# One line of transfers for two steps at once, gates turned by VectorE, and a new order of the first chunk in an mLSTM cell with a leaky-ReLU feed-forward

## The chip, the cores and the metric

The kernel runs on one core of a Trainium2 chip. The metric is the device time of one execution in microseconds (us); 484.99 us is the median of three runs of the kernel before. A core has five engines, each with an instruction stream of its own that it works through in order: TensorE (PE; loads of its weights are listed apart, as PEld), VectorE (DVE), ScalarE (ACT), GpSimd (POOL) and SyncE (SP). SyncE only gives out transfers; ScalarE can give them out too. Sixteen DMA engines carry them.

## The reference

```python
# q, k, v, o_gate: (4, 8, 768, 40); i_gate, f_gate: (4, 8, 768), all float32
for t in range(S):
    m_new = np.maximum(f_gate[:, :, t] + m, i_gate[:, :, t])
    f_stab = np.exp(f_gate[:, :, t] + m - m_new)
    i_stab = np.exp(i_gate[:, :, t] - m_new)
    C = f_stab * C + i_stab * outer(v_t, k_t)          # per batch and head, 40 x 40
    n = f_stab * n + i_stab * k_t
    h_tilde = C @ q_t
    denom = np.maximum(np.abs(n @ q_t), 1.0)
    y[:, :, t] = sigmoid(o_gate_t) * h_tilde / denom
x = y.transpose(0, 2, 1, 3).reshape(3072, 320)
h = x @ w_in                                           # w_in: 320 x 2048, float64
out = np.maximum(0.01 * h, h) @ w_out                  # w_out: 2048 x 320, float64
```

The recurrence is an attention with decays, so that it can be worked in chunks: scores inside a chunk, and a state that carries the earlier ones.

## The kernel before, in words

**Tiling.** The 768 tokens are cut into six chunks c of 128; a chunk has four steps, one for each batch entry, so there are 24 steps, s = 4c + b, of 128 tokens by 8 heads. The feed-forward of a chunk's 512 tokens is a *group* g; the loop over c runs the cell of chunk c together with group c - 1. Chunk 0 and the start of group 0 are written out in `first_chunk` (L1124). From L1244 on, a loop goes through the units of the group (`ffs`; 28 a chunk from group 1 on, 32 in group 0) and puts the parts of the cell between them at places given by lists (`place`, `first_pairs`, `pairs`, L1235 to L1239): `u_parts` (scores and state), `u_plain` (chunk 1) or `u_mix` (chunks 2 to 5; output of a step), `u_gates` (turned gates) and `u_x` (turned x, chunk 1). Group 0 multiplies in full (L812, L834); groups 1 to 5 multiply in blocks with fewer products (L976, L869).

**Order.** TensorE, VectorE, ScalarE and GpSimd run in the order in which the program names their instructions (`manual_schedule`, L1215). SyncE does not: class `Ordered` (L90) ties each transfer to the one before it only while `order["on"]` is true, that is to the end of the loads at L1229; after it every transfer is only behind that last one, and a planner orders them.

**Weights.** w_in and w_out come as 64-bit floats. `load_weights` (L234) fetches a raw block (n = 0 to 3: w_in; 4 to 11: two rows of blocks of w_out each) and `narrow_weights` (L269) makes 32-bit floats of it in six instructions: two on ScalarE (L277, L278), four on VectorE (L279 to L286). Unit j of group 0 needs block j // 2 of w_in. In the opening, blocks 0 and 1 are narrowed whole.

**Opening.** Transfers, in order: gates, then k, q, v of steps 0 and 1, block 0, o of steps 0 and 1, gates of chunk 2, k and q of steps 2 and 3, block 1, v and o of steps 2 and 3. The work of a step of chunk 0: exponentials of the gate biases that TensorE sums (L443, L459; L468, L477), turned k and q (`u_transpose`, L597, L600), scores (L609, L613), values (L700), denominators, tanh of the output gate (`prep_o`, L530), gating (L709, L713), turned x (`u_x`, L800 to L802) and the state (L621, L629). Two units of group 0 (`ffs[0]`, `ffs[1]`) stand in the midst of it.

**Gates.** `gates` (L295) scans the gates of a chunk on VectorE, `gates_exp` (L323) makes exponentials and writes the decays to DRAM (`a_dr`), `gates_T` (L346) turns them on TensorE (tile tg; L350, and L355 for the decays at the ends of the halves, spread over all partitions) and copies them with VectorE (L357, L359).

**Transfers of chunks 2 to 5.** A step's k, q and o are fetched in four transfers each (`load_blocks`, L401) into `rb_t[s % 2]`, its decays in two into `ea` (`spread_q`, L429, two buffers), all as soon as the step two before has used its own (`load_next`, L536). `u_mix` writes x of a step to DRAM in four transfers (L774) and `gather_x` (L777) fetches it back into xT in eight. k, the decay mask w and the four pieces of v of a step four ahead are given out by ScalarE, one behind each unit (`feed_slowly`, L1102). For chunk 1, `feed` (L1095) does it on SyncE.

Of the kernel before, what the change touches and what calls it, by code (L numbers as in the profile page):

```python
# [19 lines left out]
def kernel(  # L20
# [28 lines left out]
    P = 128  # L49
# [13 lines left out]
    TS = SL // QW  # L63
    RL = PR * TB * D
    RW = RL + 2 * QW
# [9 lines left out]
    SLOTS = ([0, 2, 4, 1, 3], [1, 3, 0, 2, 4])  # L75
# [13 lines left out]

    class Ordered:  # L90
# [4 lines left out]
        def dma_start(self, to, part):  # L95
            ins = self.eng.dma_start(to, part).ins  # L96
            if "at" in order:
                tc.add_manual_dep(ins, order["at"], ISSUED, reason="issue order")
            if order["on"]:
                order["at"] = ins.name  # L100

# [7 lines left out]
    for r in range(RG):  # L109
        nc.scalar.dma_start(f0[ts(r, BH), :], f_all[:, :P])  # L110
        sync.dma_start(i0[ts(r, BH), :], i_all[:, :P])
    fi = {}

    def load_fi(c):
        t = fi[c] = wk.tile([BH, 2, P], F32, name="fi")
        eng = nc.scalar if c < 2 else sync
# [22 lines left out]
    NR = 2  # L139
    EAB = 2  # L140
# [4 lines left out]
    rb_t = [consts.tile([P, 3, RW], F32, name=f"rb{n}") for n in range(NR)]  # L145
# [27 lines left out]
    def prepare_tiles():  # L173
# [4 lines left out]
        for t in rb_t:  # L178
            nc.gpsimd.memset(t[:, :, RL:], 0.0)

# [23 lines left out]
    def run_of(r, at):  # L204

        ks = SLOTS[r][at:]
        return ks[0], next((i for i in range(1, len(ks)) if ks[i] != ks[i - 1] + 2), len(ks))
# [26 lines left out]
    def load_weights(n, half=None):  # L234
# [7 lines left out]
        if half == 1:  # L242
            to = raws[n][0] if wide else dst
        elif wide:
# [12 lines left out]
        if n < QN:  # L257
            src = moe_w_in[:, n * QC : (n + 1) * QC].rearrange("(k p) (r c) -> r p k c", p=DP, r=2)
            for at, n_k in ((0, 2), (3, 2), (2, 1)):
                for r in range(2) if half is None else (half,):  # L260
                    k0 = SLOTS[r][at]
                    rows = to[DP * r : DP * (r + 1), 2 * P * at : 2 * P * (at + n_k)].rearrange("p (k c) -> p k c", k=n_k)
                    part = src[r, :, k0 : k0 + 2 * n_k - 1 : 2, :]
# [5 lines left out]
    def narrow_weights(n):  # L269
# [3 lines left out]
        raw, dst = raws.pop(n)  # L273
        words = raw.bitcast(U32).rearrange("p (c two) -> p c two", two=2)
        lo, hi = words[:, :, 0], words[:, :, 1]
        d = dst.bitcast(U32)
        yield nc.scalar.activation(dst, hi.bitcast(F32), AF.Abs)  # L277
        yield nc.scalar.activation(lo, lo, AF.Copy, scale=2.0**-29)  # L278
        yield nc.vector.tensor_scalar(  # L279
# [6 lines left out]
        yield nc.vector.tensor_tensor(d, d, lo, op=ALU.add)  # L286
# [3 lines left out]
    x_dr = dr.tile([NS, Dm, P], F32, name="x_dr")  # L290
# [32 lines left out]
    def gates_exp(c):  # L323
# [10 lines left out]
        if c > 0:  # L334
            sync.dma_start(a_dr[c, 0].rearrange("u n t -> n u t"), a[:].rearrange("n (u t) -> n u t", u=2))
            if c > 1:
                sync.dma_start(a_dr[c, 1].rearrange("u n t -> n u t"), bu[:, 2, :].rearrange("n (u t) -> n u t", u=2))
            if 1 < c < NB - 2:
# [1021 lines left out]
```

## Time and profile before

| | us |
|---|---|
| median of the three runs | 484.99 (484.12 to 487.19) |
| the profiled execution, its own time | 481.97 |
| its span, first to last instruction | 480.2 |
| TensorE busy | 463.2 |
| VectorE, ScalarE, GpSimd busy | 332.0, 203.9, 164.7 |
| DMA queues' share of 16 engines: SyncE's (q1), ScalarE's (q10) | 47.8%, 9.2% |

The profile is of one execution. Each digit of a row of slices is the busy share of a fortieth of the span (12 us) in tenths; PEclk is the clock granted to TensorE in tenths. The chain that ended last is followed back from the last instruction, step by step, to what released it. A timeline row has start, time, engine, line, operation, tiles and, in brackets, how long the engine idled before it and what ended that. L12 is line 12 of the kernel before.

### The profile page before, as it was taken

The numbers are of one execution on the slowest core, as the hardware profiler recorded it, in microseconds if no ns is written. First come the engines' busy times: TensorE is split into PE (matmuls) and PEld (weight loads), VectorE is DVE, ScalarE is ACT, GpSimd is POOL, SyncE is SP. The second block draws the span as 40 slices with busy tenths as digits, with TensorE's granted clock in tenths as the row PEclk, the third lists the DMA queues.
The fourth block names the chain that finished last, engine by engine and source line by source line (L and its number), as shares of the span: only waits on it lengthen the run. The fifth ranks groups of instructions, "written<-read, shape, count | busy, mean of one in ns | idle before, by whom it ended". The sixth has DMA issues, their size and how long they took to land.

```text
span 480.2 us, 14140 instructions
## 1 busy us (share of the span) xinstructions
PE 463.2 (96%) x5715; PEld 418.3 (87%) x5715; DVE 332.0 (69%) x588; ACT 203.9 (42%) x488; POOL 164.7 (34%) x201
## 2 busy tenths in 40 slices
PE   7586999999999999999999999999999999999997
PEld 6475888777788999988899988899988899988997
DVE  4668576798939998878698768689757686104631
ACT  3662598864336621347520446411357411153210
POOL 4232405552362333854115943114733004400020
PEclk9888899999999999999999999999999999999999
DMA  9999776968761593675673875754776112100001
GB/s 117 168 196 222 134 205 141 266 122 180 165 151 29 143 184 73 154 165 131 167 143 85 175 160 116 188 110 108 172 156 133 48 37 75 63 1 1 8 9 42
DMA packets 165329, 59.31 MB, mean 124 GB/s; under 512 B 128592, under 2 KB 156048, under 8 KB 165264
## 3 DMA queue, kind: packets, MB, share of 16 engines
q1 hardware_dynamic: 125232, 51.23, 47.8%
q10 hardware_dynamic: 40032, 7.18, 9.2%
q8 instruction: 45, 0.74, 0.6%
q14 instruction: 20, 0.16, 0.1%
HBM read 51.68 MB, written 6.70 MB: 122 GB/s over the span
## 4 chain that ended last, share of the span: by engine, by line
PE 87%; DVE 4%; SPq 4%; DMA 2%; POOL 1%; issue 1%; ACT 1%; ACTq 0%; DVEq 0%; POOLq 0%
PE ph L976 33%; PE po L869 32%; PE po L834 7%; PE ph L812 6%; SPq L96 4%; PE pT L753 3%; PE sd L665 3%; PE sd L671 1%; DMA qn<-in_q_dram 1%; DMA fi<-in_f_gate_dram 1%; PE hN L725 1%; DVE w_in L286 1%; DVE w_out L286 1%; PE tk L583 0%; DVE w_out L285 0%
## 5 line engine op out<-in xcount | busy, mean ns | idle before, releaser
L869 PE MATMUL po<-w_out,acts 128*128 128x160 f32 x640 | 89.1, 300 | 0.0
L869 PEld LDWEIGHTS po<-w_out,acts 128*128 128x128 f32 x640 | 87.3, 190 | 0.6 <-ACT acts L1001 0.3
L976 PE MATMUL ph<-xT,w_in 64*128 64x256 f32 x720 | 82.7, 378 | 0.0
L976 PEld LDWEIGHTS ph<-xT,w_in 64*128 64x128 f32 x720 | 69.2, 187 | 8.6 <-issue 0.6
L869 PE MATMUL po<-raw,acts 128*128 128x160 f32 x480 | 66.4, 300 | 0.0
L1005 DVE TENSOR_TENSOR acts<-acts,ph 128x512 f32<-128x512 f32 x60 | 38.4, 683 | 39.8 <-PE ph L976 39.6
L869 PEld LDWEIGHTS po<-raw,acts 128*128 128x128 f32 x480 | 65.4, 190 | 0.3
L641 POOL TENSOR_TENSOR S<-S,f 40x336 f32<-40x336 f32 x36 | 31.1, 864 | 67.0 <-PE pT L753 33.2
L1009 ACT COPY acts<-ph 128x512 f32<-128x512 f32 x60 | 32.2, 588 | 46.4 <-PE ph L976 46.4
L1001 ACT ACTIVATE acts<-acts 128x1024 f32<-128x1024 f32 x30 | 31.7, 1057 | 43.8 <-DVE acts L1005 40.5
L494 ACT ACTIVATE w<-w,gT 128x64 f32<-128x64 f32 x160 | 41.9, 340 | 11.3 <-POOL vu L514 3.6
L682 DVE TENSOR_TENSOR qn<-w,sd 64x384 f32<-64x384 f32 (+1 forms) x80 | 33.4, 418 | 16.4 <-ACT acts L1009 7.3
L486 POOL TENSOR_TENSOR w<-w,i 128x512 f32<-128x512 f32 x20 | 27.1, 1366 | 50.7 <-DMA w<-a_dr 23.7
L812 PE MATMUL ph<-xT,w_in 64*128 64x256 f32 x320 | 38.8, 396 | 1.6 <-DVE w_in L286 1.6
L812 PEld LDWEIGHTS ph<-xT,w_in 64*128 64x128 f32 x320 | 32.8, 196 | 5.4 <-ACT kqT L600 1.2
L834 PE MATMUL po<-w_out,acts 128*128 128x320 f32 x128 | 36.7, 437 | 0.0
L976 PE MATMUL ph<-acts,w 64*128 64x256 f32 x320 | 36.3, 379 | 0.0
L767 POOL TENSOR_TENSOR xb<-xb,den 128x320 f32<-128x320 f32 x16 | 11.6, 728 | 67.6 <-DVE xb L764 67.6
L976 PEld LDWEIGHTS ph<-acts,w 64*128 64x128 f32 x320 | 30.6, 187 | 3.6
L907 POOL TENSOR_TENSOR y<-y,raw 128x160 f32<-128x160 f32 x10 | 12.9, 1291 | 57.2 <-ACT y L906 57.2
L834 PEld LDWEIGHTS po<-w_out,acts 128*128 128x128 f32 x128 | 23.5, 190 | 9.2 <-issue 0.3
L557 DVE TENSOR_TENSOR qn<-kqT,ea 64x512 f32<-64x512 f32 x32 | 29.3, 917 | 0.8
(175 smaller groups left out, 721.1 us busy)
## 6 DMA issues: line engine op xcount, KB each, us to landing
rb<-in_k_dram SPq DMA_DIRECT2D x64, 80.0 KB
rb<-in_q_dram SPq DMA_DIRECT2D x64, 80.0 KB
rb<-in_o_gate_dram SPq DMA_DIRECT2D x64, 80.0 KB
ea<-a_dr SPq DMA_DIRECT2D x32, 128.0 KB
raw<-in_moe_w_out_dram SPq DMA_DIRECT2D x6, 640.0 KB
w<-a_dr ACTq DMA_DIRECT2D x24, 128.0 KB
xT<-x_dr SPq DMA_DIRECT2D x32, 96.0 KB
x_dr<-x SPq DMA_DIRECT2D x64, 40.0 KB
```

What stands on the lines that cost most here:

```text
L486: nc.gpsimd.tensor_tensor(w, w, cm2.unsqueeze(1).to_broadcast([P, H, SL]), op=ALU.add)
L494: yield nc.scalar.activation(w[:, h, :], w[:, h, :], AF.Exp, bias=gT[c][:, 0, bh : bh + 1], scale=1.0)
L557: nc.vector.tensor_tensor(mixed(s)[rows, 1 - r], d["kqT"][rows, 1].rearrange("p (h t) -> p h t", t=SL), d["ea"][rows], op=ALU.mult,)
L641: nc.gpsimd.tensor_tensor(new, old, g, op=ALU.mult)
L682: nc.vector.tensor_tensor(mixed(s)[toks, u, hs], w[toks, hs], bank[1 - u][to[u][hs.start], hs], op=ALU.mult,)
L812: nc.tensor.matmul(ph[r][:, cols], lhsT=w_row(r, slot, j), rhs=xT[DP * r : DP * (r + 1), slot, cols], start=(slot == 0), stop=(slot == KC ...
L834: nc.tensor.matmul(po[n][:], lhsT=acts[:, f, ts(n, P)], rhs=w_out[:, f, :], start=(f == 0), stop=(f == NF - 1),)
L869: nc.tensor.matmul(bank[:], lhsT=left[:, f, :], rhs=right[:, f, :], start=f == 0, stop=f == KH - 1)
L976: nc.tensor.matmul(bank[r][:, e, :], lhsT=left(r)[rows, e], rhs=right(r)[rows], start=first and e == 0 and m == 0, stop=e == 1 and m == le ...
L1001: nc.scalar.activation(to, z, AF.Prelu, alpha=0.01)
L1005: nc.vector.tensor_tensor(to[:, 2 * r : 2 * r + 2], to[:, 2 * r : 2 * r + 2], bank[r], op=ALU.add)
L1009: nc.scalar.copy(to[:, 2 * r : 2 * r + 2], bank[r])
```

## The change

Six things are done together.

1. **Two steps at once.** `rb` is one tile that holds k, q and o of two steps side by side. `load_blocks` fetches both steps in one transfer, when the second of them (odd s) asks; `spread_q` fetches `ea` for both, into one buffer; x of two steps goes to a common DRAM block and comes back in three transfers (the slots of xT are renumbered so that neighbours are contiguous). `feed_pair` replaces `feed_slowly`: k and w of two steps in one transfer each, the eight pieces of v as before.
2. **All on SyncE, in source order.** `order["on"]` stays true from chunk 2 on as well; ScalarE gives out transfers only at the very start. So that the order fits, `later(units, fn)` writes a transfer so many units behind the place in the source where it was: the stores of x two, the gathers four or one, the output's stores one, the gates' two, the loads of a pair one. In chunks 0 and 1 it does nothing.
3. **Gates turned by VectorE.** For chunks 2 to 5 `turn_gates` turns two kinds of gates by four 32-wide turns of VectorE; the decays at the halves' ends go through DRAM (`g_dr`) and are fetched for all partitions by `spread_decays`. Chunk 1 keeps `gates_T`. `u_gates` is gone from the list of cells.
4. **First chunk.** Its steps are cut into small ones (`turn`, `turned`, `scores`, `scaled`, `values`, `dens`, `gated`, `normed`, `ends`, `flip`, `flipped`, ...) that run in the order of one long string. Blocks 0 and 1 of w_in are narrowed in two halves each (by `e`, so that a unit needs one half), their low words on ScalarE into a place of their own (`narrow_low`). Three units of group 0 stand in it instead of two. Six warming matmuls at the start are gone, four and two stand further on. Some gating moves to GpSimd. The transfers are in a new order, given before the rest.
5. **Group 0.** A new order of transfers for chunk 1, with v of steps 4 to 7 in one transfer each to a place in `acts` from which GpSimd copies the halves (`split_v`); new places of the cells; a list of how many narrowing instructions run at each unit (`now`).
6. **Chunk 2.** Slightly other places of cells, of the mixed weights and of the gates (`pr`, `mix`, `ga`, `ge`).

The diff, cut to its core:

```diff
-    SLOTS = ([0, 2, 4, 1, 3], [1, 3, 0, 2, 4])
+    SLOTS = ([0, 1, 2, 3, 4], [1, 2, 3, 4, 0])
...
+    def later(units, fn):
+        if unit[0] is None or units == 0:
+            fn()
+        else:
+            due.append((unit[0] + units, fn))
...
-            if "at" in order:
-                tc.add_manual_dep(ins, order["at"], ISSUED, reason="issue order")
             if order["on"]:
+                if "at" in order:
+                    behind(ins, order["at"])
                 order["at"] = ins.name
+            else:
+                behind(ins, order["at"])
...
-    rb_t = [consts.tile([P, 3, RW], F32, name=f"rb{n}") for n in range(NR)]
+    rb = consts.tile([P, 3, RW], F32, name="rb")
...
+    def low_part(n, e):
+        at = (WC // 2 * e, 4 * HW * 2)[n]
+        return raw_l[:, at : at + WC // 2].bitcast(U32).rearrange("p (k c) -> p k c", k=KC)
+    def narrow_low(n, e):
+        words = raws[n][0].bitcast(U32)
+        lo = words.rearrange("p (k e c two) -> p k e c two", k=KC, e=2, two=2)[:, :, e, :, 0]
+        nc.scalar.activation(low_part(n, e), lo, AF.Copy, scale=2.0**-29)
...
+    def spread_decays(c):
+        to = f0[:, ts(c % 2, 2 * BH)]
+        sync.dma_start(to, g_dr[c].rearrange("n u -> (n u)").partition_broadcast(P))
+        gL[c] = to.rearrange("p (n u) -> p u n", u=2)
+    def turn_gates(c):
+        bu = bus.pop(c)[0]
+        g = gT[c] = wk.tile([P, 3, BH], F32, name="gT")
+        for j in range(P // BH):
+            nc.vector.transpose(g[ts(j, BH), :2, :], bu[:, :2, ts(j, BH)])
...
+    def split_v(s):
+        halves = staged(s).rearrange("p (h k d) -> p h k d", k=2, d=DB)
+        for u in range(2):
+            nc.gpsimd.tensor_copy(S_v[s % NL][ts(u, SL), u, :, :, :DB], halves[ts(u, SL)])
...
-        elif s < NS:
-            load_blocks(s, i)
+        elif s < NS and s % NR:
+            load_blocks(s - 1, i)
...
-        src = (k, q, o_gate)[i][b, :, ts(c, P), :]
+        src = (k, q, o_gate)[i][b : b + NR, :, ts(c, P), :].rearrange("b h p d -> (b h) p d")
...
+        if s % NR == 0:
+            return
...
-        d["ea"] = wk.tile([P, H, SL], F32, name="ea", bufs=EAB)
+        ea = wk.tile([P, NR * H, SL], F32, name="ea", bufs=1)
...
-        if s + NR < NS:
+        def fetch():
             load_late(s + NR, 0)
             load_late(s + NR, 1)
             if s + NR >= 2 * B:
                 spread_q(s + NR)
+        if s + NR < NS:
+            later(1, fetch)
...
+        later(2, out_x)
...
-        src = x_dr[s].rearrange("(k p) t -> p k t", p=DP)
+        src = x_dr[s // NR].rearrange("(k p) m t -> p k (m t)", p=DP)
...
-            send(n, 1)
+            later(0 if last else 1, lambda: send(n, 1))
...
-    def feed_slowly(steps):
...
+    def feed_pair(s, eng):
...
+        yield eng.dma_start(
+            kn[:, n : n + NR, :, :D].rearrange("p m h d -> p (m h) d"),
+            k[b : b + NR, :, ts(c, P), :].rearrange("b h p d -> p (b h) d"),
+        )
+        for m in range(NR):
+            for u in range(2) if m else ():
+                yield eng.dma_start(
+                    w_all[ts(u, SL), n : n + NR, : H * SL],
+                    a_dr[c, 0, u, b * H : (b + NR) * H, :].rearrange("(m h) t -> m (h t)", m=NR).partition_broadcast(SL),
+                )
...
+    ORDER = "gates:0 masks:0 gexp:0 terms:0 exps:0:1 gT:0 gates:1 exps:0:1 exps:0:1 exps:0:1 masks:1 vu:0 turn:0:0 turn:1:0 turn:0:1 turned:0:0:v turned:0:1:s turned:1:0:s scores:0 turn:1:1 scaled:0:0 terms:1 exps:1:2 exps:1:2 exps:1:2 scaled:0:1 narrow:0:1:1 o:0 turned:1:1:v scores:1 scaled:1:0 low:0:0 scaled:1:1 values:0 values:1 narrow:0:0:1 gexp:1 gated:0 dens:0 o:1 dens:1 normed:0:v ends:0:s narrow:0:0:1 flip:0 gated:1 normed:1:g exps:1:2 begin warm:4 narrow:0:1:1 flipped:0:1:s narrow:0:1:1 narrow:0:0:1 turn:2:0 exps:1:2 ends:1:g narrow:0:0:1 vu:1 turned:2:0:v tiles flipped:0:0:s narrow:0:0:1 step:1 low:0:1 flip:1 turn:2:1 exps:1:2 exps:1:2 flipped:1:0:s flipped:1:1:v narrow:0:1:1 turned:2:1:s turn:3:0 ff:0 narrow:0:1:1 exps:1:2 scores:2 turn:3:1 turned:3:1:s state:0 low:1:1 state:1 narrow:1:0:1 scaled:2:1 low:1:0 scaled:2:0 turned:3:0:v vu:2 step:0 kept:0 scores:3 kept:1 narrow:1:0:1 values:2 o:2 narrow:1:1:1 narrow:1:0:1 gT:1 vu:3 ff:1 gated:2 scaled:3:0 narrow:1:1:1 scaled:3:1 warm:2 dens:2 normed:2:g narrow:1:1:1 narrow:1:0:1 ends:2:g narrow:1:0:1 o:3 values:3 step:2 dens:3 flip:2 gated:3 normed:3:g ends:3:s ff:2 flip:3 narrow:1:1:1 flipped:2:0:s state:2 flipped:2:1:s flipped:3:0:s step:3 state:3 narrow:1:1:1 kept:3 kept:2 flipped:3:1:s".split()
...
+        for line in "0:1 1:0 0:0 1:1 0:2 8:0 1:2 0:3 2:0 1:3 2:2 2:1 3:1 3:0 3:3 8:1 2:3 3:2 9:2".split():
+            n, i, *at = map(int, line.split(":"))
+            if n == 9:
+                load_fi(i)
+            elif n == 8:
+                load_weights(i, *at)
+            else:
+                load_first(n, i)
         ffs = first_chunk()
...
+        for line in "f:5:0 l:4:2 l:4:1 w:2 f:4:1 f:5:1 l:5:1 f:4:0 f:4:2 w:3 f:7:1 w:4 f:5:2 f:6:1 f:7:0 f:6:0 w:5 w:6 f:7:2 l:5:2 f:6:2".split():
...
+        Z = {'nff': 3, 'fetch': {7: (3,), 9: (5, 6), 10: (4,), 16: (7,)}, 'place': (6, 8, 11, 12, 14, 16, 18, 20, 20, 22, 23, 28), 'now': [0, 1, 4, 0, 1, 2, 4, 1, 1, 2, 3, 5, 3, 4, 3, 3, 3, 4, 3, 2, 4, 3, 5, 5], 'ahead': 3, 'sums': 23, 'g1': 0, 'e1': 6, 'chain': 1, 'sv': (0, 3, 10, 10), 'np': (), 'mix': (3, 6, 10, 11), 'ga': 0, 'ge': 5, 'pr': (1, 1, 3, 3, 12, 14, 17, 17), 'gt': 11}
...
+                if c > 1:
+                    unit[0] = 0 if unit[0] is None else unit[0] + 1
+                    for job in [job for job in due if job[0] <= unit[0]]:
+                        due.remove(job)
+                        job[1]()
...
+                    if i == (Z['e1'] + 4, Z['ge'] + 4, 7)[min(c, 3) - 1]:
+                        spread_decays(c + 1)
+                    if i == (Z['gt'], 10, 10)[min(c, 3) - 1]:
+                        turn_gates(c + 1)
...
-                    for s in waiting:
-                        gather_x(s)
+                    for s in waiting:
+                        later(4 if s % B > 1 else 1, lambda s=s: gather_x(s))
...
-                            if fn is u_mix:
-                                slow.append(s + NL)
-                            else:
-                                feed(s + NL)
+                            if fn is u_mix and s % NR:
+                                chores.append(feed_pair(s + NL - 1, sync))
+                            elif s % NR:
+                                for _ in feed_pair(s + NL - 1, sync):
+                                    pass
```

In the order of the opening's transfers, a pair n:i is step n's q, k, v or o (i = 1, 0, 2, 3), 8 is a block of weights and 9 the gates of a chunk; in that of group 0, f:s:0, f:s:1 and f:s:2 are k, v and w of a step, l:s:1 and l:s:2 its q and o, w:n a block of weights.

More of the change, by code (lines that the diff above doesn't have):

```diff
@@ L88, with behind @@
     order = {"on": True}
+    def behind(ins, name):
+        tc.add_manual_dep(ins, name, ISSUED, reason="issue order")
+    due, unit = [], [None]
+    def later(units, fn):
[3 more added lines that the diff above has]
+            due.append((unit[0] + units, fn))
     class Ordered:
@@ L241, in load_weights @@
         to = dst
[L242 to L244 removed]
+        if wide:
             if n < 2:
@@ new lines, in exps, with feeds, begin @@
+        def exps(g, n):
+            run(e[g], n)
+        def feeds(j):
+            t["ff"][j]()
+        def begin():
+            t["ff"] = ff_units(0)
+        steps = {
+            "gates": gates, "gexp": gates_exp, "warm": warm, "masks": masks, "terms": terms, "gT": lambda c: gates_T(c, bus[c][0]),
+            "vu": prep_vu, "turn": turn, "turned": turned, "scores": scores, "scaled": scaled, "values": values, "dens": dens,
+            "gated": gated, "normed": normed, "flip": flip, "flipped": flipped, "ends": ends, "narrow": narrow, "low": narrow_low, "exps": exps, "o": prep_o,
+            "ff": feeds, "state": state, "kept": state_copy, "tiles": prepare_tiles, "step": prepare_step, "begin": begin,
+        }
@@ L1292 @@
                         del fine[min(fine)]
-                if c == 1 and i >= 24:
+                if c == 1 and i >= Z['sums']:
                     run(sums, 1)
-                if c == 2 and i in (3, 4, 11, 12):
+                for _ in range(Z['mix'].count(i - n_ff) if c == 1 else Z['mix'].count(i) if c == 2 else 0):
                     next(mixes)
```

374 lines of the change are left out of this document (187 added, 187 removed).

## The prediction

> **What bounds the kernel now.** I read the page's summary first, then its 40 slices, then the chain that ended last, then one table by windows for the opening, TensorE's timeline there, and the waits of SyncE's queue.
>
> ```profile
> PE 463.2 (96%) x5715; PEld 418.3 (87%) x5715; DVE 332.0 (69%) x588; ACT 203.9 (42%) x488; POOL 164.7 (34%) x201
> PE   7586999999999999999999999999999999999997
> PEclk9888899999999999999999999999999999999999
> PE 87%; DVE 4%; SPq 4%; DMA 2%; POOL 1%; issue 1%; ACT 1%; ACTq 0%; DVEq 0%; POOLq 0%
> ```
>
> From the fifth slice on TensorE is full at full clock, and 87% of the chain is TensorE. Holes are in the first four slices (48 us). After that only work taken off TensorE can shorten the kernel, or a new wait lengthen it.
>
> ```profile
> 12.00:24.00 12.00, 7.08 (x127) 5.65 (x125) 8.12 (x23) 7.82 (x20) 2.70 (x9) 0.83 1.01 168
> 24.00:36.00 12.00, 10.13 (x116) 9.10 (x118) 7.60 (x12) 7.90 (x18) 4.34 (x11) 0.88 1.12 196
> 36.00:48.00 12.00, 8.19 (x132) 6.78 (x130) 9.83 (x23) 2.89 (x8) 2.45 (x8) 0.83 1.07 222
> 48.00:60.00 12.00, 12.00 (x154) 10.76 (x152) 6.05 (x11) 6.93 (x16) 4.93 (x5) 0.89 0.78 134
> ```
>
> The columns are PE, PEld, DVE, ACT and POOL busy, then the granted clock, the DMA share and GB/s. TensorE idles and loses clock while the DMA engines are full: the opening is set by transfers and by the order of small steps together.
>
> ```profile
> 22.62 0.66 PE L800 MATMUL xt<-ident,x 128*128 128x128 f32 x2 [4.73 <-DVE x L713]
> 43.47 0.41 PE L800 MATMUL xt<-ident,x 128*128 128x128 f32 x2 [2.25 <-DVE x L713]
> 46.55 10.93 PE L812 MATMUL ph<-xT,w_in 64*128 64x256 f32 x80 [0.86 <-DVE w_in L286]
> 180.46 0.24 PE tg L350 x2
> 180.71 0.12 PE tg L355 x2
> SPq L96 <- DVE x L771: 23.3, 10, 10.0
> SPq L96 <- DVE y L928: 21.0, 4, 15.0
> ```
>
> The first three rows are TensorE's timeline (start, time, idle before and what ended it), the next two the chain in order of time, the last two SyncE's waits (us, times, longest). The waits of TensorE before 46.55 add up to 13.0 us (1.47, 0.94, 0.19, 4.73, 0.78, 1.08, 0.69, 2.25, 0.86). The 80 records at 46.55 are four units of group 0; they take 10.93 us. 60 records at 58.5 take 6.75, or 2.25 a unit, so the half clock (0.50 from 44 on) costs these four 1.9 us. Those four end at 57.5: that is the mark I measure the opening by, with six units done.
>
> **The change, part by part.**
>
> *The opening.* I lay the new written order out with durations from rows, every engine taking its list in order. f0 has landed at 4.24; the gates take VectorE 1.31 (4.24 to 5.55). The bias terms took 2.0 at full clock (6.04 to 8.04); twelve warming matmuls that ran ahead of them are removed, so I take 3.4, the factor 1.7 by the transposes L597 (1.06 against 0.60). To 9.1. Four exponentials at 0.51 (L468, 2.06 for four): 11.2. Masks 0.96, three transposes at 0.52: 13.8. A copy on ScalarE 0.55, scores 1.12, transpose 0.52, terms 1.1: 17.2. Six exponentials at 0.275: 18.9.
>
> Then data: the first weights were used at 19.34 after six loads of 160 KB; one now goes behind them, at 1.08 us (six in 6.5 us, about 4.2 to 10.7), so 18.3, just not late. Step 0's output gate comes next but one, about 19.8. Behind it on ScalarE: tanh 0.43, two half conversions at 0.70 (the 640-wide rows of L277 and L278), gate exponentials 1.2, tanh 0.43, a copy 0.25, with the gaps 23.6. TensorE then turns x 0.97, warms 1.0, transposes 0.52, turns x 0.97 and transposes twice at 0.52; the copies of x let the first unit run 28.3 to 30.6. In before it ran 27.65 to 30.08: no gain yet.
>
> After it come scores 1.12, a transpose 0.52 and two states at 0.55 to 33.3; a copy 0.64 and scores and values 2.2 to 36.2; gates 0.42; the second unit to 38.9. Here VectorE leads: halves of the second weights (0.50, 0.50, 0.83, 0.83, the 640-wide rows of L279 to L286) lie between scaling, sums and gating, and end at 42.1. The third unit ends at 44.4, x of step 3 and two states at 46.5. In before everything of chunk 0 was turned at 45.7, with two units done, not three.
>
> Three more units at 2.25 end at 53.3 with six done, against 57.5: **4.2 us gained**: the extra unit (2.3) and the clock (1.9). The splitting costs VectorE 5.2 against 4.6 us a weight block; that is in the list. If the landing of the output gate cost nothing, the list would end at 44.8, gain 5.9; with half clock until 13.2 at 47.2, gain 3.5. I take 4.2, since ScalarE did wait for a transfer here (L277, 2.77 us).
>
> *Group 0's transfers.* All stay on SyncE, in a written order, with the keys and values of steps 4 to 7 partly ahead of the third and fourth weight blocks. Filled from 33.4 (step 5's keys must wait for step 1's state, 33.3): three loads, a block at 6.0, four loads and 2 us to land put step 4's keys at 49.7; they are first used after two more units, 46.5 + 4.5 = 51.0. By the same count the fourth block lands at 56.8 (wanted 56.6), the first two of w_out at 63.5 and 73.5 (63 and 74). So nothing is late by more than 0.2, and nothing has slack either: I cost it at 0, bounds 0 and 4.2 (the whole head start given back). Steps 4 to 7's values as one 160 KB load each (1.08 against four of 40 KB) plus eight GpSimd copies lie in GpSimd's idle time (0.79 us busy from 60 to 72); nearest row L739, 0.24 to 0.71 each. The cells' new places move no wait: TensorE's only one in group 0 (1.04 at 92.28, for GpSimd's ku) lies between step 5's end at unit 12 and step 6's start at 14, and both stay there.
>
> *Gates turned by VectorE.* Four times (102.6, 180.5, 250.9, 321.2) the five transposes of tg leave TensorE's chain: 0.24 + 0.12 = 0.36 each, **1.4 us**. VectorE gets four 32-wide turns for two copies (0.23, 0.21); the nearest row is the 128x512 transpose L549, 0.70, so 0 to 2.4 more a chunk, and VectorE has about 15 us idle in each 70 (55.2 busy, 205 to 275). The decays' trip through DRAM is given two units, 5 us, before it is fetched.
>
> *Two steps at once, all on SyncE.* For chunks 2 to 5 SyncE issued 352 (rb 192, ea 32, x 64 out and 64 back) and ScalarE 84 (w 24, kn 12, S 48). Now SyncE issues 266: rb 96, ea 16, x 64 and 24, w 12, kn 6, S 48, at 0.4 to 0.6 each some 130 us of 346. ScalarE loses 84 issues it had time for. No TensorE wait went with them, so the gain is 0. The cost is order: behind a waiting issue now stand the next chunk's w, kn and S too, and a pair's k, q and ea, which may start only when the second step's are read. In the chunk seen, those were read at 205.9 and are next wanted at 223.4: 17.5 us. One step's set was issued in 6.0 (213.5 to 219.5) and two with 2 us to land take 14: 3.5 to spare. I take 0; bounds 0 and the hold below.
>
> Sum: 4.2 + 1.4 = 5.6. The profiled execution took 481.97 (span 480.2, and 1.8 around it), so 476.4; on the median, 3.0 higher, **484.99 - 5.6 = 479.4**. A measurement of this kernel tells about 1% (4.85 us) from no change.
>
> **A rule against it.** The row first: the granted clock fell to 0.50 at 20 after TensorE had idled from 17.9 to 22.6, and again at 43.9 around a gap of 2.25. The Trainium skill, "TensorE: Matmul & The Clock Gate", section "What's actually happening", has half rate as the default, full rate after a busy window of about 3.4 us and half again after an idle one, windows running free. The rows agree. It makes one rival, the second below.
>
> **The rivals.**
>
> 1. *More than the list: the waits go.* Against it, VectorE was busy 9.83 of 12 us from 36 to 48; for it, 13.0 us of waits. If 10 of them go: 484.99 - 10 - 1.4 = 473.6. Chance 0.13.
>
> 2. *The clock falls in the new gaps.* My list leaves TensorE idle from 21.2 to 23.6 and before 5.7. The price is the 1.9 of four units at half clock, once more: 481.3. Four warming matmuls stand there against it. Chance 0.09.
>
> 3. *Weights late in group 0.* With no slack, ScalarE waits in its line (it waited 5.95 us for w_out at 115.6) and with it the activations that free PSUM. The 4.2 are lost: 483.6. Chance 0.16.
>
> 4. *A hold in the one line of SyncE.* The next chunk's w is issued at units 9 and 10 and its mask is due at 14: 4 units, 10 us at 70.3/28. The longest hold of SyncE in before was 15.0 (y L928); then w lay on ScalarE's queue. If such a hold stands ahead of w, GpSimd's mask, ScalarE's exponentials and TensorE's scores come 5 us late, in each of three chunks: 479.4 + 15 = 494.4, slower. It decides from a hold over 10 us. Against it: the stores are now issued one or two units after the work that they wait for. Chance 0.15.
>
> 5. *As forecast*, 479.4, own range 476 to 481.5. Chance 0.47.
>
> The range takes in 1 to 3 and the forecast, and of 4 the shorter holds, to 8 us over the forecast: 473 to 488. Faster by over 1% is below 480.1: all of 1 and about 0.38 of 5's 0.47, 0.51. Within 1%: 2, 3 and the rest of 5, 0.34. Slower: 4, 0.15.
>
> **What would show it.** The opening: three units before chunk 0 is done, the sixth over near 53.3, clock 1.0 from about 44 on. Group 0: no TensorE idle before the split of step 4 (now L583), ScalarE's waits for weights under 1 us. Gates: no tg but the first two, chunks at about 69.9 instead of 70.3 us. SyncE: waits for DVE under 5 us each, and no TensorE wait behind GpSimd's mask. The prediction is wrong if chunks 2 to 5 are longer than 70.3, or if TensorE's sum of waits in the opening stays near 13.

## The result

| | before | after |
|---|---|---|
| median of six runs, us | 485.69 (483.70 to 487.19) | 498.21 (497.15 to 500.76) |
| ratio, 95% interval | | 1.0273 (1.0234 to 1.0312) |
| profiled execution, its own time / span | 481.97 / 480.2 | 500.76 / 498.9 |

The change makes the kernel 2.7% slower: outside the forecast range of 473 to 488, and the other way than forecast. The medians differ by 12.5 us, the spans of the two profiled executions by 18.7: that of the kernel before was 3.7 faster than the median of its six runs, that of the changed one the slowest of its six. The stretches below therefore overstate the loss by some 6 us in all, and single ones are read only together with the experiments. To place the 18.7 us I read five starts of TensorE's products in the timeline: the seventh unit of group 0 (the six before it and the split of step 4 are done), the first product of group 1, and the first products of groups 2 to 5.

| stretch | before | after | difference |
|---|---|---|---|
| start to seventh unit of group 0 | 58.44 | 53.59 | -4.85 |
| from there to group 1 | 75.65 | 86.16 | +10.51 |
| group 1 (with chunk 2) | 72.61 | 85.46 | +12.85 |
| groups 2 and 3 (chunks 3 and 4) | 140.49 | 140.32 | -0.17 |
| group 4 (chunk 5) and group 5 | 132.99 | 133.35 | +0.36 |
| sum | 480.18 | 498.88 | +18.70 |

So in these two executions the opening gained about what was forecast (4.2), and two places lost five times as much.

### The profile after

The page's summary and slices of the changed kernel, then its chain:

```profile
PE 469.8 (94%) x5699; PEld 421.2 (84%) x5699; DVE 333.0 (67%) x602; ACT 202.2 (41%) x493; POOL 170.0 (34%) x209
PE   6799998999799998399999999999999999999997
PEclk9899999999799999699999999999999999999999
GB/s 123 172 173 190 225 195 70 227 184 108 164 154 16 103 79 199 103 157 193 46 178 159 107 219 121 80 203 98 170 201 98 4 54 59 75 2 1 8 7 41
PE 76%; SPq 8%; DVE 6%; DMA 5%; issue 2%; POOL 2%; ACT 0%; ACTq 0%; DVEq 0%; POOLq 0%
```

TensorE is no longer full behind the fourth slice: the eleventh (125 to 137 us) has 7 tenths, the seventeenth (200 to 212) has 3, both with a lower clock. The chain now runs 8% over SyncE's queue and 5% over transfers, where 87% of it was TensorE. In the row of GB/s, the seventh slice (75 to 87 us) moves 70, though group 0's loads are due there. The windows of these stretches (columns: PE, PEld, DVE, ACT, POOL busy, granted clock, DMA share, GB/s):

```profile
74.00:78.00 4.00, 4.00 (x84) 3.38 (x83) 3.68 (x4) 3.85 (x12) 3.88 (x5) 1.00 1.36 44
78.00:82.00 4.00, 3.47 (x83) 2.71 (x73) 3.73 (x10) 1.71 (x5) 2.07 (x3) 1.00 0.53 24
82.00:86.00 4.00, 2.43 (x96) 2.21 (x98) 1.98 (x8) 2.53 (x6) 0.76 (x1) 1.00 0.43 62
86.00:90.00 4.00, 4.00 (x27) 3.02 (x28) 3.90 (x5) 3.90 (x9) 3.75 (x5) 1.00 1.03 227
...
170.00:174.00 4.00, 3.99 (x91) 3.52 (x89) 3.90 (x8) 1.96 (x5) 0.00 (x0) 1.00 0.37 25
174.00:178.00 4.00, 4.00 (x30) 3.14 (x31) 3.97 (x7) 2.06 (x2) 0.00 (x0) 1.00 0.27 12
```

From 75 to 85, and from 170 to 178, hardly anything moves, though from 78 on the DMA engines count as a quarter to half busy: the same few packets are under way for long (the 2560-byte packets of w_out took up to 8.3 us each; in the kernel before, 1.1). SyncE's queue in these places (start, time, transfer, count):

```profile
73.36 0.76 SPq L110 DMA_DIRECT2D g_dr<-bu  x1
...
76.89 12.61 SPq L110 DMA_DIRECT2D raw<-in_moe_w_out_dram  x3
...
104.24 2.16 SPq L110 DMA_DIRECT2D rb<-in_k_dram  x4
```

```profile
168.70 0.60 SPq L110 DMA_DIRECT2D g_dr<-bu  x1
...
170.49 5.53 SPq L110 DMA_DIRECT2D S<-in_v_dram  x3
178.26 0.35 SPq L110 DMA_DIRECT2D f<-g_dr  x1
...
180.10 4.60 SPq L110 DMA_DIRECT2D rb<-in_k_dram  x4
184.81 2.92 SPq L110 DMA_DIRECT2D rb<-in_q_dram  x4
187.83 1.34 SPq L110 DMA_DIRECT2D ea<-a_dr  x2
189.22 1.81 SPq L110 DMA_DIRECT2D w<-a_dr  x2
```

The store `g_dr<-bu`, the 64 decays of a chunk, stands 1 to 2 us ahead of each stretch. Two losses follow. In group 0, one issue of w_out is held from 76.89 to 87.42, and everything behind it with it: keys and queries of steps 8 and 9 are given out at 104 to 112, VectorE stands in its line for them, and w_out is narrowed too late for TensorE. In chunk 2 the decay masks w are issued at 189.22; in the kernel before, ScalarE's queue issued the first at 162.2. VectorE's, GpSimd's and TensorE's timelines show both losses (the bracket is idle time and what ended it):

```profile
113.73 0.71 DVE L621 STREAM_TRANSPOSE kqT<-rb 128x512 f32<-128x512 f32 x1 [4.89 <-DMA rb<-in_k_dram]
117.31 0.71 DVE L621 STREAM_TRANSPOSE kqT<-rb 128x512 f32<-128x512 f32 x1 [2.86 <-DMA rb<-in_q_dram]
```

```profile
128.56 8.56 PE L919 MATMUL po<-w_out,acts 128*128 128x320 f32 x20 [3.53 <-DVE w_out L322]
```

```profile
197.20 2.48 POOL L555 TENSOR_TENSOR w<-w,i 128x512 f32<-128x512 f32 x2 [31.18 <-DMA w<-a_dr]
```

```profile
207.45 7.30 PE L954 MATMUL po<-raw,acts 128*128 128x160 f32 x32 [9.18 <-DVE acts L1008]
```

GpSimd holds the mask in its line for 31.18 us. By the chain that ended last, what stands behind it comes late too: the state (S) and gating (xb) on GpSimd, then x and acts on VectorE. TensorE's products of group 1 wait 9.18 us for acts, and its clock is halved from 202.7 to 213.0. In group 0 it is halved from 127.6 to 134.5, around the wait of 3.53.

### The profile page after: what moved, and what is told of

It is laid out like the page before. It is cut to its first block, busy times and chain, and to the rows that moved or that the text cites. A ratio compares the mean times of both kernels' runs of the same rounds, so it can differ in the third digit from the quotient of the medians.

```text
span 498.9 us, 13835 instructions
## 1 busy us (share of the span) xinstructions
PE 469.8 (94%) x5699; PEld 421.2 (84%) x5699; DVE 333.0 (67%) x602; ACT 202.2 (41%) x493; POOL 170.0 (34%) x209
## 3 DMA queue, kind: packets, MB, share of 16 engines
q1 hardware_dynamic: 152624, 58.44, 62.5%
## 4 chain that ended last, share of the span: by engine, by line
PE 76%; SPq 8%; DVE 6%; DMA 5%; issue 2%; POOL 2%; ACT 0%; ACTq 0%; DVEq 0%; POOLq 0%
PE ph L1061 32%; PE po L954 30%; SPq L110 8%; PE po L919 4%; PE pT L827 3%; PE ph L897 3%; PE sd L737 3%; DMA w<-a_dr 1%; DMA acts<-in_v_dram 1%; DMA rb<-in_q_dram 1%; PE hN L796 1%; DMA qn<-in_q_dram 1%; PE sd L743 1%; DVE w_out L321 1%; DVE w_out L322 1%
## 5 line engine op out<-in xcount | busy, mean ns | idle before, releaser
L954 PEld LDWEIGHTS po<-w_out,acts 128*128 128x128 f32 x640 | 87.4, 190 | 0.9 <-DVE acts L1090 0.3
L954 PE MATMUL po<-raw,acts 128*128 128x160 f32 x480 | 69.4, 308 | 9.2 <-DVE acts L1008 9.2
L954 PEld LDWEIGHTS po<-raw,acts 128*128 128x128 f32 x480 | 68.1, 196 | 9.7 <-issue 9.4
L1090 DVE TENSOR_TENSOR acts<-acts,ph 128x512 f32<-128x512 f32 x60 | 38.4, 683 | 39.0 <-PE ph L1061 38.9
L713 POOL TENSOR_TENSOR S<-S,f 40x336 f32<-40x336 f32 x36 | 29.0, 806 | 53.7 <-PE pT L827 28.2
L919 PE MATMUL po<-w_out,acts 128*128 128x320 f32 x128 | 39.6, 463 | 4.0 <-DVE w_out L322 4.0
L919 PEld LDWEIGHTS po<-w_out,acts 128*128 128x128 f32 x128 | 25.2, 203 | 15.4 <-DVE w_out L322 5.0
L992 POOL TENSOR_TENSOR y<-y,raw 128x160 f32<-128x160 f32 x10 | 10.4, 1049 | 57.8 <-ACT y L991 57.8
```

The source lines that it names most:

```text
L713: nc.gpsimd.tensor_tensor(new, old, g, op=ALU.mult)
L919: nc.tensor.matmul(po[n][:], lhsT=acts[:, f, ts(n, P)], rhs=w_out[:, f, :], start=(f == 0), stop=(f == NF - 1),)
L954: nc.tensor.matmul(bank[:], lhsT=left[:, f, :], rhs=right[:, f, :], start=f == 0, stop=f == KH - 1)
L1090: nc.vector.tensor_tensor(to[:, 2 * r : 2 * r + 2], to[:, 2 * r : 2 * r + 2], bank[r], op=ALU.add)
```

## The experiments

Two theories. **G**: the store g_dr itself stalls the DMA engines. **L**: the loss is made by SyncE's one line, in which w stands behind the pair's values. A third possibility (**C**) was that the stretches without packets are chance or belong to the new order of loads.

### 1. w ahead of the values

The edit, in words:

```diff
 feed_pair(s), from chunk 3's first pair on:
   kn (both steps)
+  w u=0, w u=1 (both steps)
   S of the first step, four pieces
-  w u=0, w u=1 (both steps)
   S of the second step, four pieces
```

> Only the order of the transfers of a pair of steps is changed, from chunk 3's first pair on: its keys, then its two w transfers, then its eight value pieces (in the changed kernel four value pieces stand ahead of w). Theory L (w stands too late in SyncE's one line: issued at 189.22, landed at 197.07, and the mask, S, acts and po behind it wait 9.2 us, then half clock): chunk 2, 85.46 us long in the changed kernel, falls to about 73 and the kernel to about 486. Rival G (the small store g_dr, 64 elements of 4 bytes, stalls the DMA engines for some 8 us after each issue, whatever stands in the line): the stretch with hardly a packet at 170 to 178 stays, w is issued at about 181 and lands near 188, chunk 2 gets at most 5 us shorter, and the kernel takes 493 or more. Group 0 (first product of group 1 at 139.82) stays within 1 us under both.

Measured: 489.12 us, ratio to before 1.0119 (1.0067 to 1.0171). Group 1 lasts 75.26 instead of 85.46; it starts at 138.43. So 10.2 us of chunk 2's loss go with the order alone, more than rival G allowed. (That group 1 starts 1.3 earlier is a little more than the 1 us that both allowed.) But the stall is still there: w, issued at 169.84, reaches GpSimd 13 us later.

```profile
182.91 3.48 POOL L555 TENSOR_TENSOR w<-w,i 128x512 f32<-128x512 f32 x2 [18.18 <-DMA w<-a_dr]
```

Neither theory has its number; both are at work.

### 2. Without the store

```diff
-                sync.dma_start(g_dr[c], bu[:, 2, :].rearrange("n (u t) -> n u t", u=2)[:, :, SL - 1])
...
-                        spread_decays(c + 1)
...
-                        turn_gates(c + 1)
+                        gates_T(c + 1, bus.pop(c + 1)[0])
```

This gives the gates' and decays' transposes, 0.36 us a chunk by the prediction, back to TensorE as well.

> The gates of chunks 2 to 5 are turned by TensorE again and the decays come from the same transposes, so the store g_dr and its fetch into f are gone; all else is as in the changed kernel. Theory G (the 64 four-byte elements stall the DMA engines): the stretch with hardly a packet at 76 to 86 goes, SyncE's issue of w_out is no longer held 10.5 us, and the first product of group 1 starts at 130 to 133 instead of 139.82; the stretch at 170 to 178 goes too and chunk 2 falls from 85.46 to 73 to 80. In all 484 to 489 with the 1.4 us of transposes paid. Rival L (the line itself, not the store): the stretches without packets stay, the group starts near 139, chunk 2 is within 2 us of 85, and the kernel takes 497 to 500.

Measured: 483.23 us, 0.9991 (0.9964 to 1.0018). Group 1 starts at 132.86 and lasts 74.34. G's numbers hold (the time is 0.8 below its range), L's don't. The same windows as above:

```profile
74.00:78.00 4.00, 4.00 (x42) 3.52 (x38) 3.67 (x4) 3.98 (x14) 3.91 (x4) 1.00 0.52 135
78.00:82.00 4.00, 2.52 (x106) 2.05 (x104) 2.58 (x6) 1.63 (x7) 3.00 (x4) 1.00 1.14 297
82.00:86.00 4.00, 4.00 (x96) 3.44 (x98) 2.96 (x10) 3.46 (x8) 0.56 (x1) 1.00 0.90 341
```

297 and 341 GB/s where there were 24 and 62; SyncE gives out the three w_out transfers in 4.27 us instead of 12.61:

```profile
76.84 4.27 SPq L110 DMA_DIRECT2D raw<-in_moe_w_out_dram  x3
```

### 3. Both

The edits of 1 and 2 together.

> Both edits of the two kernels before it together. If store and order each cost what their theory says and nothing else was lost, group 1 starts at 130 to 133 and chunk 2 takes 70.3 to 72: 478 to 482. If the two are one loss seen twice, the time is that of the better of the two alone. If the opening's 5 us are given back elsewhere (the pair of steps 8 and 9 fetched too late for VectorE's line), group 1 starts at 134 or later and the time is 483 to 486.

Measured: 481.47 us, 0.9964 (0.9947 to 0.9981), inside 478 to 482. Group 1 starts at 132.14, as expected, but takes 73.22, over the 70.3 to 72 expected. With the four kernels the two causes can be told apart:

| | store g_dr | no store |
|---|---|---|
| w behind the values: kernel / group 1's stretch | 498.21 / 85.46 | 483.23 / 74.34 |
| w ahead | 489.12 / 75.26 | 481.47 / 73.22 |

Late w alone costs group 1 1.1 us, the stall alone 2.0, both 12.2: the stall delays the whole line, and only where w also stands behind the values does it come far too late for GpSimd's line. Over the whole kernel the store costs 15.0 or 7.7 us, the order 9.1 or 1.8 (the first of the four was timed beside 485.69 for the kernel before, the other three beside 483.87).

### 4. The store alone, in the kernel before

```diff
+    g_dr = dr.tile([NB, BH, 2], F32, name="g_dr")
...
+                sync.dma_start(g_dr[c], bu[:, 2, :].rearrange("n (u t) -> n u t", u=2)[:, :, SL - 1])
```

The store stands behind the stores of `a_dr` in `gates_exp` of the kernel before; nobody reads it.

> The kernel before, with only the store g_dr added behind the two a_dr stores of chunks 2 to 5; nobody reads it. Theory G: a stretch of 3 to 10 us with hardly a packet follows each of the four stores, the instruction fetches in it take 3 to 6 us instead of 1.3, SyncE's issues are held there, and the kernel gets slower, by 2 to 10 us where a stretch meets loads without slack (group 0). Rival C (the stretches are chance, or come with the new order of transfers): none is seen, and the time stays within 1 us of the kernel before.

Measured: 507.47 us, 1.0498 (1.0428 to 1.0569): 23.6 us slower, more than twice what I allowed. None of the other changes is in this kernel, so order, pairs and the fetch of the decays are not needed for the stall. Windows behind its first store (issued at 78.33):

```profile
78.00:82.00 4.00, 4.00 (x120) 3.42 (x118) 1.13 (x1) 3.92 (x12) 2.86 (x3) 1.00 0.50 38
82.00:86.00 4.00, 3.98 (x46) 3.22 (x42) 3.42 (x8) 2.65 (x7) 0.00 (x0) 1.00 0.33 14
86.00:90.00 4.00, 1.17 (x24) 0.94 (x24) 1.55 (x4) 0.97 (x3) 0.28 (x1) 0.94 0.32 16
90.00:94.00 4.00, 1.78 (x62) 1.70 (x60) 3.53 (x7) 0.04 (x1) 3.21 (x5) 0.50 0.91 326
```

The kernel before moved 338 GB/s from 82 to 86:

```profile
82.00:86.00 4.00, 4.00 (x116) 3.40 (x114) 3.75 (x7) 2.23 (x6) 0.76 (x1) 1.00 0.99 338
```

With the store it is 14, and 16 in the next 4 us; then TensorE's clock is halved as well. Behind the second store (170.62) the windows 174 to 178 and 178 to 182 moved 10 and 6. Two of TensorE's waits have no releaser in the profile:

```profile
PE sd L667 <- issue: 6.9, 1, 6.9
...
PE hN L727 <- issue: 2.8, 1, 2.8
```

"Issue" is time in which TensorE waited for nothing that the profile shows. The wait of 2.8 ends at 88.83, that of 6.9 at 187.91, in the first and just behind the second of the stretches with few packets. Transfers that bring in instructions (16 KB packets on a queue of their own) are held up too: 4.0 us for one that starts at 80.37, and up to 6.1 in the changed kernel, where the longest in the kernel before took 1.6. But that TensorE waited for its own code isn't shown: the packet of 4.0 us had ended 4 us before the wait of 2.8 did, and the only one seen during the wait of 6.9 (it starts at 185.40) took 1.0. What TensorE waited for stays open.

### 5 and 6. What about the store stalls

The same 64 elements from the same tile at the same place, once with 64 bytes each, once with 4 bytes each but 256 bytes from one another:

```diff
 5: g_dr = dr.tile([NB, BH, 2, 16], F32, name="g_dr")
+   sync.dma_start(g_dr[c], bu[:, 2, :].rearrange("n (u t) -> n u t", u=2)[:, :, SL - 16 :])
 6: g_dr = dr.tile([NB, BH, 2, SL], F32, name="g_dr")
+   sync.dma_start(g_dr[c, :, :, SL - 1], bu[:, 2, :].rearrange("n (u t) -> n u t", u=2)[:, :, SL - 1])
```

> The kernel before with a store added at the same place as in the kernel before plus g_dr, from the same tile, of the same 64 elements, but each of 64 bytes instead of 4; nobody reads it. If what stalls is the write of a few bytes, there are no stretches without packets and the time is within 1 us of the kernel before (483.9), against 507.5 with 4 bytes. If what stalls is one more store at this place, or its wait in SyncE's line, it takes 500 or more again.

> The kernel before with the 64 elements of 4 bytes again, but each 256 bytes away from the next in DRAM; nobody reads them. If what stalls is that 64 writes meet in the same 256 bytes of DRAM, the stretches go and the time is within 2 us of 483.9. If any write of 4 bytes stalls, it takes 500 to 510 as with the 64 packed together.

Measured: 484.92 us, 0.9996 (0.9959 to 1.0033), and 484.55, 0.9991 (0.9950 to 1.0031). Neither costs anything that could be told from nothing. It is not the number of elements, nor the place in the line, nor small writes as such, but small writes that lie close together in DRAM.

The Trainium skill, "DMA: Bandwidth & Descriptors", "Specifications", says that transfers under 512 bytes make the DMA engine read, change and write back. No run here shows that step. By size alone, elements of 4 bytes 256 apart would have to cost as much as packed ones; they cost nothing, so size alone does not make the stall.

### 7. Decays by VectorE too

```diff
+        gL[c] = f0[:, ts(c % 2, 2 * BH)].rearrange("p (u n) -> p u n", u=2)
+        for j in range(P // BH):
+            for u in range(2):
+                last = SL * (u + 1) - 1
+                nc.vector.transpose(gL[c][ts(j, BH), u, :], bu[:, 2, last : last + 1].to_broadcast([BH, BH]))
```

This stands in `turn_gates`, on top of w ahead; the store, its fetch and the transposes on TensorE are left out.

> The changed kernel with w ahead of the values, and the decays made by VectorE as the gates are: eight turns of 32 by 32 of the one column, repeated, straight into f; no store g_dr, no fetch of it, no transposes on TensorE. Against the version with w first and TensorE's transposes (481.47): the five transposes and their bank of PSUM are gone, 0.36 us in each of four chunks, and the wait of 1.5 us for VectorE's copy at 80. If only the transposes counted: 480.0. With the wait at 80 gone too: 478.6. If the eight turns more (some 2 us of VectorE a chunk by the 0.97 for four) are on the path of group 0, where VectorE has the least idle time, 481.5 to 483.

Measured: 486.70 us, 1.0026 (0.9983 to 1.0068): 5 us slower than with TensorE's transposes, and outside all that I wrote. Eight turns at 0.18 us and four at 0.23 are 2.4 us of VectorE in one go. TensorE's waits now have a new line:

```profile
PE ph L1065 <- DVE acts L1094: 2.7, 3, 1.2
```

Groups 2 and 3 take 71.62 and 71.39 instead of 70.60 and 70.63. VectorE is 70% busy over the span, but the go of 2.4 us comes in the line that also makes acts, for which TensorE waits here. Group 1 takes 1.5 more. The rest of the difference lies before group 1 (135.01 against 132.14), of which the profiled opening alone was 1.3 late (a wait of 3.1 for the keys of a step). For the other 1.6 the trace shows two waits for ScalarE behind the turns, 1.10 at 83.39 and 1.37 at 85.04, and half clock from 84.9 to 88.3; experiment 3 has neither there, but a wait of 1.47 for the copy. What each of them costs was not tried.

### 8. Free order on SyncE

Experiment 2 with `order["on"] = False` from group 1 on.

> The version without the g_dr store (gates and decays by TensorE, w behind the first values: 483.23), but from chunk 2's group on SyncE's issues are no longer held to source order: the scheduler places them as in the kernel before, pairs and delays kept. If source order alone costs something (a load behind a store that waits), chunk 2 falls from 74.3 to near 72.6 and the time to 480 to 482. If the order costs nothing once the store is gone, it stays within 1.5 us of 483.2. If the scheduler's order lets the stores with long waits come first, it gets slower, 486 or more.

Measured: 482.27 us, 0.9956 (0.9925 to 0.9988), 1.0 below experiment 2. Group 1 takes 73.69 against 74.34. The intervals overlap: source order by itself is no loss that could be told from nothing.

### 9 and 10. The change with its store mended

Gates by VectorE as in the change (0.97 us a chunk), decays by two transposes on TensorE and one copy, w ahead of the values; in 10 SyncE's order is free as well.

```diff
-                sync.dma_start(g_dr[c], bu[:, 2, :].rearrange("n (u t) -> n u t", u=2)[:, :, SL - 1])
...
+    def turn_decays(c):
+        bu = bus[c][0]
+        tg = psc.tile([P, 2, BH], F32, name="tg", tag="c")
+        for u in range(2):
+            last = SL * (u + 1) - 1
+            nc.tensor.transpose(tg[:, u, :], bu[:BH, 2, last : last + 1].to_broadcast([BH, P]), ident[:BH, :BH])
+        gL[c] = f0[:, ts(c % 2, 2 * BH)].rearrange("p (u n) -> p u n", u=2)
+        nc.vector.tensor_copy(gL[c], tg[:])
...
-                        spread_decays(c + 1)
...
+                        turn_decays(c + 1)
                         turn_gates(c + 1)
```

> The changed kernel with w ahead of the values, gates turned by VectorE (0.97 us for four in one go) and the decays by two transposes on TensorE (0.12 us) with one copy on VectorE: no g_dr. Against TensorE's five transposes (481.47, chunks 3 and 4 at 70.60): if VectorE's turns are free, as the forecast had it, chunks 3 and 4 fall to 70.2 to 70.3 and the kernel to 480 to 481. If a go of 1 us on VectorE at that place makes TensorE wait for a sum (as the eight turns more did: 2.7 us in three waits, chunks 71.6), chunks stay at 70.6 or more and the time at 481.5 to 483.

> The same with SyncE's issues from group 1 on placed by the scheduler instead of in source order. If source order costs nothing once store and w are mended, within 1 us of the run beside it. If it costs the 0.6 us by which chunk 2 was longer than in the kernel before (73.2 against 72.6), chunk 2 falls to about 72.6.

Measured: 481.30 us, 0.9937 (0.9909 to 0.9966), and 481.71, 0.9945 (0.9921 to 0.9970). Both are below the kernel before by 0.6%, and well below the changed one; from experiment 3 they can't be told. Groups 2 and 3 take 70.46 and 70.37, between the two expectations: the four turns of VectorE are nearly free, the eight more of experiment 7 were not. In 10 group 1 takes 73.60, in 9 73.55: the order is not what keeps it 1 us above the kernel before. One more reading of 9, SyncE's waits:

```profile
SPq L110 <- DVE x L854: 79.6, 16, 17.1
```

In the slower changed kernel this line read 69.8 us, longest 16.7. The kernel of experiment 9, 17 us faster, has *more* of it. Its hold of 17.1 us (133.7 to 150.8) is followed by no wait of TensorE in group 1.

### 11 and 12. How near, and how many

The kernel before with 64 elements of 4 bytes 64 bytes from one another, and with only 16 elements, packed in 64 bytes.

```diff
 11: g_dr = dr.tile([NB, BH, 2, 16], F32, name="g_dr")
+    sync.dma_start(g_dr[c, :, :, 15], bu[:, 2, :].rearrange("n (u t) -> n u t", u=2)[:, :, SL - 1])
 12: g_dr = dr.tile([NB, BH, 2], F32, name="g_dr")
+    sync.dma_start(g_dr[c, :8], bu[:8, 2, :].rearrange("n (u t) -> n u t", u=2)[:, :, SL - 1])
```

> The kernel before with the 64 stores of 4 bytes at 64 bytes from one another in DRAM (256 apart was free, 484.55; packed cost 507.5). If the clash is between writes to the same 64 bytes, it is free here too: within 2 us of 484. If it is between writes to the same larger block (256 bytes or more), a part of the stall is seen: 490 to 500, four writes to each 256 bytes instead of 64.

> The kernel before with only 16 of the 64 four-byte elements stored, packed in 64 bytes. If the stall is a sum over writes to the same place, each some 0.1 us, the stretches shrink to a quarter, 1 to 2 us each, which the kernel's slack partly hides: 484 to 490. If any clash stalls for a fixed time, it is 500 or more, as with 64.

Measured: 483.40 us, 0.9983 (0.9951 to 1.0016), and 484.99, 1.0018 (0.9991 to 1.0044). 64 bytes apart is free. With 16 packed the window 82 to 86 is full again, and it is the length of the stall that has shrunk: the longest packets of other loads behind the first two stores took 2.1 and 2.2 us, against 5.5 and 4.2 with 64 (one of instructions 2.7 against 4.0).

```profile
82.00:86.00 4.00, 4.00 (x82) 3.40 (x82) 3.69 (x9) 2.99 (x7) 0.16 (x1) 1.00 0.96 326
```

An estimate from experiment 4: packets come back about 11 us after the end of the issue at 78.98, so 64 elements cost some 0.17 us each, one after the other; 16 would be 2.7, which fits, and which this kernel's slack hides. But with 16 elements the stretch of DRAM shrank too, from 256 bytes to 64, so that the cost goes by the number of elements is not shown. Whether pitches between 4 and 64 bytes stall, and what in the memory or the DMA engines makes the stall, wasn't tried.

## Why the prediction was wrong

**The step that failed** is the last sentence of "Gates turned by VectorE": "The decays' trip through DRAM is given two units, 5 us, before it is fetched." It asked only whether the trip is early enough and put no price on the store itself. "0 to 2.4 more a chunk" was a bound for VectorE alone. The profile of before had no store of 4-byte elements; behind its nearest rows, the stores of a_dr with 256-byte elements, no packet of w_out took over 1.1 us. I should have bounded the new kind of transfer from above too. It measured 23.6 us in the kernel before (four stores), and 15.0 or 7.7 in the changed one.

**The opening** was right in size: forecast 4.2 (six units done at 53.3 instead of 57.5); in the two profiled executions the seventh unit starts 4.85 earlier. The other profiled executions bear it out: in five kernels with the old opening and no harmful store (before, 5, 6, 11, 12) it starts at 59.3 on average (57.99 to 60.39), in five with the new one (2, 3, 8, 9, 10) at 54.4 (53.35 to 55.41), 4.9 earlier. Three units stood in it as said, and TensorE's waits up to 47 us fell from 13.0 to 8.1 (10.0 to 10.8 in experiments 2, 3 and 9). The clock was wrong in detail: it was halved twice, from 21.8 to 25.2 and from 35.5 to 38.9, and 1.0 from then to 127.6. So **rival 2** did happen in part, within a list that ended in time; the time at half clock fell from 13.7 us (20.0 to 26.8, 43.9 to 50.7) to 6.8. The four spells at half clock of the changed kernel last 3.41, 3.41, 6.83 and 10.24 us. The Trainium skill, "TensorE: Matmul & The Clock Gate", "What's actually happening", gives a free-running window of 3.413 us; the trace agrees, with one, one, two and three of them.

**Group 0's transfers**, "nothing is late by more than 0.2, and nothing has slack either": the second half was the true one. In the changed kernel one issue was held 10.5 us, and the stretch from the seventh unit to group 1 took 86.16. Experiment 2 takes 78.94, so 7.2 of the 10.5 lost there go with the store, and 3.3 are lost without it. Without the store, **rival 3** took a part of what it was priced at: the mean start of group 1 is 135.4 in the five old kernels (134.09 to 137.16) and 132.4 in the five new ones (131.42 to 133.41), so of 4.9 us 3.0 are left. Some of the missing 1.9 is the wait of rival 3 (TensorE for ScalarE's relu behind the fourth block of weights: 0.83 in the changed kernel, 1.42 in experiment 2), some is the wait of 1.5 for VectorE's copy of the decays in 2, 3, 8 and 9, which TensorE does not have in the kernel before. The forecast "ScalarE's waits for weights under 1 us" failed by itself, 2.42 at 59.02.

**Gates**: 1.4 us were to come off TensorE. Chunks 3 and 4 took 70.04 and 70.28 against 70.29 and 70.20 before, 0.17 for two, where 0.72 were forecast; VectorE's turns cost 0.97 a chunk, inside the bounds. Experiment 9 against 3 gives 0.40 for the same two chunks; there three transposes, 0.24 in all, are gone from each and two are kept, so 0.48 was due. The mechanism fits; why the changed kernel gained only 0.17 of its 0.72 was not shown.

**Two steps at once, all on SyncE**: costed at 0 with the hold as upper bound. The 17.5 us for a pair's reads were enough: no later chunk waits. Source order is worth nothing either way (8, 10). That chunk 2 stays about 1 us longer (73.2 to 73.6 against 72.6) was not settled.

**Rival 4** had the right start of the chain (w late, GpSimd's mask late), the right place and nearly the right condition: a hold over 10 us ahead of w. Three things were off. The hold came not from a store that waits for VectorE but from transfers that were held up. Behind the mask the delay ran through S, xb, x and acts, not through ScalarE's exponentials and the scores. And it hit one chunk, in which it cost 12, not 5 in each of three: in chunks 3 and 4 the windows behind the store are as empty (31 and 10 GB/s from 240 to 248, 20 and 23 from 310 to 318), but w goes out 27.5 and 28.2 us after the group's first product instead of 49.5, and TensorE does not wait. The rival's time, 494.4, at a chance of 0.15, was the nearest of all, but partly by luck: 10.5 us of the loss lie in group 0, of which it says nothing. It also misread SyncE's waits: the longest hold of the kernel before was 37.8 (`y L899`), not 15.0, and both are at the stores of the output near the end (416 to 454 and 456 to 471 us), with no next chunk behind them. The test that I gave for it ("SyncE waits for DVE under 5 us each") was a bad one, as experiment 9 shows.

With the store mended and w ahead of the values, the forecast of 5.6 us came out as 2.8 (experiment 9 against the kernel before on the same chip, 481.30 and 484.12).

## What to carry to other kernels

Price a new transfer by its elements and where they land, not by its bytes: a store of 256 bytes as 64 packed elements of 4 cost more than any other edit here, and the same store with the elements 64 bytes apart cost nothing. In one line of transfers ask of each what stands ahead of it when something stalls, and send first what is due first; a long wait behind it was harmless here. When a kernel has lost time in two far places, look for what precedes both before explaining each, and try the suspect alone in the old kernel.

## What the runs showed of the hardware that I had not expected

- A store of 64 packed 4-byte elements to DRAM holds up nearly all the core's DMA traffic, loads of other tensors and instruction fetches too: 14 to 16 GB/s for 8 us in experiment 4, 507.47 against 483.87 us with four such stores. With 16 packed elements the longest packets of loads took 2.1 and 2.2 us and the kernel 484.99; with 64 elements 64 or 256 bytes apart, or of 64 bytes each, there is no stall (483.40, 484.55, 484.92).
- In and just behind two such stretches of experiment 4 TensorE waited 6.9 and 2.8 us for nothing that the profile shows; for what, stays open.
- Turns of VectorE on 32 x 32 blocks take 0.18 us each with a repeated column as source, 0.23 on 32 x 64. With twelve in a row TensorE had new waits of 2.7 us in all for VectorE (experiment 7), with four it had none (experiment 9).
